# A new written order for the opening and the first 60 half blocks of an attention kernel with two expert layers

## The chip, the cores and the metric

The kernel runs as one program on one core of a Trainium2 chip. The metric is the device time of one execution in microseconds. Before the change it was 1586.91 us, the median of three runs that lay between 1586.84 and 1587.07 us.

The core has a matrix engine (PE in the profile), a vector engine (DVE), an activation engine (ACT), a general engine (POOL) and a queue that issues all transfers here (SP). Each engine works through its own instructions strictly in order, so the order in which the program lists them decides what waits behind what.

## The reference

The input is q, k, v of 8 batches, 8 heads, 576 tokens and 64 channels, and phi with 32 memory slots. The reference, cut to what is computed:

```
a    = softmax over the tokens of phi                # 8 x 8 x 576 x 32
k_m  = a^T k ;  v_m = a^T v                          # 32 rows for each head
attn = softmax over the slots of (q k_m^T / 8)
x    = attn v_m          -> 4608 tokens x 512
h    = x w_in  (512 -> 2048);  x = (h - tanh h) w_out      # layer 1
h    = x w_in2 (512 -> 2048);  x = elu(h) w_out2           # layer 2
```

The four weight matrices arrive as 64-bit floats.

## The kernel before

**Attention.** The work of 4 heads of one batch is a *unit*; there are 16 (u0 to u15), written as a generator `unit` (L251 to L370) that is advanced one step at a time. Its steps are in turn: the negated maximum of phi (DVE, L270); the exponential (ACT, L272); transposes aT and tail on PE (L278, L280) and their copies into tile `a` (L282 on DVE or L284 on ACT, L285 on ACT); the products km on PE (L294, L298); their scaling into kvs (L308 on ACT or L310 on DVE); the transposes kT (PE L317) and two copies (ACT L318, L320); the scores sc (PE L334) and their transposes (DVE L337); the maximum over the slots (DVE L341) and its subtraction (L342, POOL or DVE); the exponential (ACT L344); the sum, its reciprocal and the product (L346, L347 on DVE, L348 on POOL or DVE); a transpose (DVE L353); the split of the result into a high and a low part (L359 on POOL or L361 on ACT, then L362 on POOL or DVE); and the store of both (SP, L366 or L368). The result is the tile p, which layer 1 reads.

**Conversions.** Each weight matrix is brought from 64 to 32 bits in 16 pieces, 64 pieces in all (c0 to c63), each by a generator `conv` (L690) around `convert` (L176): a load of 512 KB (L693); a magnitude on ACT (L187); a clip (L189) on DVE or POOL; three steps of bit work on DVE (L192, L195, L198); and, save for the first matrix, a split into high (L204 on POOL or L206 on ACT) and low (L208 on POOL). The first matrix's pieces go into tiles named w1 in the lists below: c0 to c3 into the two that the first two half blocks need, c8 to c11 into the two that the next two need.

**Layer 1.** Tokens are cut into 16 blocks of 288 and the hidden width into groups of 256. Attention's last product and the first matrix are multiplied together first (`vw_unit`, L430: PE L440, then a copy on ACT L444 and a rest on DVE L445), so a hidden tile is p times vw (PE L458, H below). A *half block* is one block with one group; there are 128. One half block's chain: H, tanh and square (ACT L469, L473), a product (POOL L482), a polynomial (ACT L477, DVE L498), the difference h - tanh h (DVE L494), a mask (ACT L489) and a masked copy that chooses between the two (DVE L502), then the split (ACT L511, POOL L516). The second matrix follows some half blocks later: 12 matmuls for each x tile (PE L531) and a copy out of PSUM, on ACT (step X, L537) or on DVE (step Y, L539). Half blocks 0 and 1 use one vw, 2 and 3 the next, and so on.

**What sets the order.** Nothing is scheduled by a program here. A written list sets the order in which instructions are emitted: `BEGIN` lists steps up to the first half block (cN and uN advance a conversion or a unit; pN, qN and kN load phi, q, or k with v of unit N; v makes the first vw), and `SCRIPT` has one string for each of the 128 half blocks. Its letters are H (matmuls of the hidden tile), A, a, s, B, R, d, e, p (the chain: L469, L473, L477, L482, L489, L494, L498, L502), G and g (the split), X and Y (one x tile with its copy on ACT or DVE), V (a new vw), L and l (loads and stores), W (no work in most places). `POOLS` has a string for each unit that moves single steps to another engine, and `WHERE` a character for each conversion:

```python
on = lambda step: nc.gpsimd if step in where else nc.vector      # L254: letters s, m, l -> L342, L348, L362
if "e" in where: nc.vector.tensor_copy(a[:, :16]..., aT)          # L281, otherwise ACT
if "k" in where: nc.scalar.activation(kvs, twice, ...)            # L307, otherwise DVE
if "h" in where: nc.gpsimd.tensor_copy(t[:, 0], src)              # L358, otherwise ACT
hi_pool, where = where in ":GSB", {":": "."}.get(where, where.lower())   # L182: high part on POOL
m = a if where in "sb" else psum.tile(...)                        # L184: bit work in SBUF or in PSUM
(nc.gpsimd if where in "gb" else nc.vector).tensor_scalar(...)    # L189: the clip
```

The hidden tiles have two PSUM buffers, so H of a half block waits until the masked copy (L502) of the half block two before has read its tile; x tiles, vw and the attention units share three other PSUM buffers. Weight pieces have five load buffers. Layer 2 (L549 to L653) follows after about 780 us and is not touched by the change.

## Time and profile before

| | us |
|---|---|
| median of three runs | 1586.91 |
| the profiled execution | 1586.47 |
| its span, first to last instruction | 1584.5 |
| PE busy | 1532.8 (97% of the span) |
| DVE busy | 1103.8 (70%) |
| ACT busy | 892.0 (56%) |
| POOL busy | 720.4 (45%) |

The span is 1.97 us shorter than the profiled execution's time, and that execution is 0.44 us under the median. PE is busy nearly throughout, and of the 51.7 us in which it is not, most lie ahead of the layer 1 stream and in its first quarter. DVE's share of 70% is a mean: in the first slices of the page it is busy seven to nine tenths, in layer 2 five to six. A matmul row's end is modelled, and rows of one engine can overlap by some hundredths of a microsecond.

### The profile page before, as it was taken

The numbers are of one execution on the slowest core, as the hardware profiler recorded it, in microseconds if no ns is written. First come the engines' busy times: TensorE is split into PE (matmuls) and PEld (weight loads), VectorE is DVE, ScalarE is ACT, GpSimd is POOL, SyncE is SP. The second block draws the span as 40 slices with busy tenths as digits, with TensorE's granted clock in tenths as the row PEclk, the third lists the DMA queues.
The fourth block names the chain that finished last, engine by engine and source line by source line (L and its number), as shares of the span: only waits on it lengthen the run. The fifth ranks groups of instructions, "written<-read, shape, count | busy, mean of one in ns | idle before, by whom it ended". The sixth has DMA issues, their size and how long they took to land.

```text
span 1584.5 us, 27123 instructions
## 1 busy us (share of the span) xinstructions
PE 1532.8 (97%) x10406; PEld 1335.4 (84%) x10406; DVE 1103.8 (70%) x1615; ACT 892.0 (56%) x1603; POOL 720.4 (45%) x516
## 2 busy tenths in 40 slices
...
GB/s 324 290 145 247 250 227 212 291 240 220 179 169 169 222 227 226 219 190 179 320 269 107 69 51 67 41 67 54 69 65 40 93 41 71 49 67 40 40 1 27
DMA packets 118593, 232.84 MB, mean 147 GB/s; under 512 B 7616, under 2 KB 77248, under 8 KB 114368
## 3 DMA queue, kind: packets, MB, share of 16 engines
...
q10 hardware_dynamic: 288, 0.52, 0.1%
...
## 4 chain that ended last, share of the span: by engine, by line
PE 85%; DVE 7%; ACT 4%; issue 1%; POOL 1%; DMA 1%; SPq 0%; ACTq 0%; DVEq 0%; POOLq 0%
PE h_ps L591 25%; PE o_ps L638 25%; PE x_ps L531 21%; PE h_ps L458 11%; PE vw_ps L440 2%; DVE s L498 1%; PE km L294 1%; DVE s L502 1%; POOL v L482 1%; ACT t L469 1%; DVE cv_m L195 0%; DVE h_ps L494 0%; ACT u L473 0%; DVE w L198 0%; DVE cv_m L192 0%
## 5 line engine op out<-in xcount | busy, mean ns | idle before, releaser
L617 POOL TENSOR_TENSOR e<-hm,e 128x512 fp32r<-128x512 f32 x144 | 186.9, 1298 | 574.9 <-ACT e L616 531.8
L531 PE MATMUL x_ps<-g,w 128*128 128x288 f32 x3072 | 433.4, 296 | 6.5 <-ACT x L537 2.7
L531 PEld LDWEIGHTS x_ps<-g,w 128*128 128x128 f32 x3072 | 414.4, 188 | 14.2 <-ACT x L537 4.6
L591 PE MATMUL h_ps<-x,wi 128*128 128x512 f32 (+1 forms) x1920 | 422.2, 370 | 0.0
L638 PE MATMUL o_ps<-wo,e 128*128 128x512 f32 x1728 | 421.7, 393 | 0.0
L591 PEld LDWEIGHTS h_ps<-x,wi 128*128 128x128 f32 x1920 | 336.1, 188 | 66.2
L638 PEld LDWEIGHTS o_ps<-wo,e 128*128 128x128 f32 x1728 | 323.3, 188 | 73.1 <-POOL e L617 0.4
L602 ACT ACTIVATE t_ps<-hm 128x512 f32<-128x512 f32 x144 | 86.7, 602 | 500.6 <-DVE hm L601 500.6
L516 POOL TENSOR_TENSOR g<-s,g 128x576 fp32r<-128x576 f32 x128 | 199.3, 1557 | 106.3 <-ACT g L511 87.1
L482 POOL TENSOR_TENSOR v<-t,u 128x576 f32<-128x576 f32 x128 | 186.3, 1455 | 118.7 <-ACT u L473 109.7
L608 DVE SCALAR_TENSOR_TENSOR hm<-hm,t_ps 128x512 f32<-128x512 f32 x144 | 98.9, 687 | 200.6 <-ACT hm L603 200.6
L458 PE MATMUL h_ps<-p,vw 128*128 128x288 f32 x1536 | 233.3, 301 | 2.5 <-DMA p<-p_dram 0.8
L458 PEld LDWEIGHTS h_ps<-p,vw 128*128 128x128 f32 x1536 | 212.4, 190 | 17.6 <-issue 10.5
L601 DVE TENSOR_SCALAR hm<-h_ps 128x512 f32<-128x512 f32 x144 | 99.5, 691 | 128.2 <-PE h_ps L591 126.9
L498 DVE SCALAR_TENSOR_TENSOR s<-s,v 128x576 f32<-128x576 f32 x128 | 128.9, 1007 | 51.5 <-ACT big L489 30.5
L469 ACT ACTIVATE t<-h_ps 128x576 f32<-128x576 f32 x128 | 83.4, 652 | 67.8 <-issue 27.6
L502 DVE COPY_PREDICATED s<-big,h_ps 128x576 f32<-128x576 uint32 x128 | 106.3, 830 | 10.0 <-ACT big L489 1.3
L477 ACT ACTIVATE s<-u,bias 128x576 f32<-128x576 f32 x128 | 99.6, 778 | 13.2 <-POOL g L516 5.0
L494 DVE TENSOR_TENSOR h_ps<-h_ps,t 128x576 f32<-128x576 f32 x128 | 97.0, 758 | 13.7 <-ACT u L473 13.6
L609 DVE SCALAR_TENSOR_TENSOR hm<-hm,t_ps 128x512 f32<-128x512 f32 x144 | 98.9, 687 | 5.0
L610 DVE TENSOR_TENSOR hm<-hm,h_ps 128x512 f32<-128x512 f32 x144 | 98.9, 687 | 5.0
L489 ACT ACTIVATE big<-u,bias 128x576 f32<-128x576 f32 x128 | 98.2, 767 | 3.2 <-DVE s L502 3.0
...
## 6 DMA issues: line engine op xcount, KB each, us to landing
x_dram<-x SPq DMA_DIRECT2D x128, 288.0 KB, 2.7
xr<-x_dram SPq DMA_DIRECT2D x72, 512.0 KB, 3.7
p<-p_dram SPq DMA_DIRECT2D x62, 576.0 KB, 5.3
kv<-in_kv_dram SPq DMA_DIRECT2D x16, 1152.0 KB, 7.3
raw<-in_moe_w_in_dram SPq DMA_DIRECT2D x32, 512.0 KB, 4.6
raw<-in_moe_w_out_dram SPq DMA_DIRECT2D x32, 512.0 KB, 4.7
w_dram<-wst SPq DMA_DIRECT2D x32, 512.0 KB, 3.8
q<-in_q_dram SPq DMA_DIRECT2D x16, 576.0 KB, 5.6
```

What stands on the lines that cost most here:

```text
L458: nc.tensor.matmul(ps[:, j, :NB], lhsT=vw[a][:, kc, c0 + 128 * j:c0 + 128 * j + 128], rhs=p[:, kc, b, :], start=(k == 0), stop=(k == 5))
L469: nc.scalar.activation(t, w[0], ACTF.Tanh)
L477: self.nc.scalar.activation(s, u, ACTF.Square, bias=self.const["bias"][:, 0:1], scale=G_S)
L482: nc.gpsimd.tensor_tensor(v, t, u, op=ALU.mult)
L498: eng.scalar_tensor_tensor(s, s, G_B, v, op0=ALU.add, op1=ALU.mult)
L502: self.nc.vector.copy_predicated(s, big.bitcast(U32), d)
L516: self.nc.gpsimd.tensor_tensor(g[:, 1], s, r32(g[:, 0]), op=ALU.subtract)
L531: nc.tensor.matmul(ps, lhsT=wo[pg][a][:, j, 128 * dm:128 * dm + 128], rhs=self.g[n, pg][:, b, j, :], start=(k == 0), stop=(k == 11))
L591: nc.tensor.matmul(out, lhsT=w3[:, a, kc, 128 * j:128 * j + 128], rhs=x[:, b, kc, :], start=(i == 0), stop=(i == 11))
L601: nc.vector.tensor_scalar(hm, w[0], 0.0, None, op0=ALU.min)
L617: nc.gpsimd.tensor_tensor(e[:, 1], hm, r32(e[:, 0]), op=ALU.subtract)
L638: nc.tensor.matmul(acc, lhsT=e[:, a, jj, 128 * tg:128 * tg + 128], rhs=w4[:, b, j, :], start=(k == 0 and jj == 0 and (a, b) == (0, 0)), st ...
```

## The change

The list is written anew from `BEGIN` to the string of half block 59; half blocks 60 to 127 keep their strings. `POOLS` and `WHERE` are new too. No function changes. Every half block keeps its letters of the chain; steps of units and conversions stand in other places, some x copies change between X and Y, and some steps change engine. Cut to the two tables and the first lines of the lists:

```diff
-BEGIN = ("c0 p1 c0 q1 p0 u1 u0 u0 c1 u0 k1 u1 p2 c0 k0 c1 c2 u1 c0 c2 u2 c1 q0 c2 u1 u0 u1 c3 c4 c6 c2 u2 u0 "
+BEGIN = ("c2 p1 p0 c2 u1 u1 u0 k1 c0 u0 c2 u1 c0 c0 c2 c0 c1 u0 k0 p2 c1 q0 q1 c1 c1 u2 u1 u1 u0 c3 u2 c4 u3 "
...
-SCRIPT = ("c6 W u2 c4 H A a d s V u0 R G Y v X L c5 B u3 l e p g c6 c7",
+SCRIPT = ("W c6 c4 Y H A a Y v L R G c5 s V u3 B d e p c5 g l",
...
-POOLS = ("sl", "mks", "lmsk", "msl", "sl", "sk", "", "e", "lk", "ls", "msk", "mlk", "m", "mlsek", "lk", "lk")
-WHERE = "..s.gb.g:ggb.g:.g.s..g:.g:g...............................gss..."
+POOLS = ("slhm", "mks", "lmske", "msl", "slkh", "sk", "h", "kmh", "", "shk", "msk", "lkh", "mkeh", "msekh", "lkme", "lk")
+WHERE = "b...gb:g.GgB.g:sg.:..gG.g:g..G............................gss.g."
```

What this does to the instructions shows in their order on single engines. In the names below a number tells one tile from another, and the same tile has another number in the two kernels.

SP, the first eleven transfers of the program, before (raw is a conversion's piece, kv_139 unit 1's and kv_157 unit 0's k and v; phi_164, phi_171 and phi_196 belong to units 1, 0 and 2):

```order
L693 DMA raw_162<-in_moe_w_in_dram 128x512
L248 DMA phi_164<-in_phi_dram 128x576
L248 DMA q_169<-in_q_dram 128x1152
L248 DMA phi_171<-in_phi_dram 128x576
L693 DMA raw_180<-in_moe_w_in_dram 128x512
L248 DMA kv_139<-in_kv_dram 128x2304
L248 DMA phi_196<-in_phi_dram 128x576
L248 DMA kv_157<-in_kv_dram 128x2304
L693 DMA raw_204<-in_moe_w_in_dram 128x512
L248 DMA phi_223<-in_phi_dram 128x576
L248 DMA q_230<-in_q_dram 128x1152
```

The same place in the changed kernel (phi_166 is unit 0's phi, phi_221 and phi_234 those of units 2 and 3):

```order
L693 DMA raw_162<-in_moe_w_in_dram 128x512
L248 DMA phi_164<-in_phi_dram 128x576
L248 DMA phi_166<-in_phi_dram 128x576
L248 DMA kv_139<-in_kv_dram 128x2304
L693 DMA raw_179<-in_moe_w_in_dram 128x512
L693 DMA raw_206<-in_moe_w_in_dram 128x512
L248 DMA kv_157<-in_kv_dram 128x2304
L248 DMA phi_221<-in_phi_dram 128x576
L248 DMA q_226<-in_q_dram 128x1152
L248 DMA q_228<-in_q_dram 128x1152
L248 DMA phi_234<-in_phi_dram 128x576
```

Unit 0's phi and unit 1's k and v now stand ahead of both q and of the second piece of weights, and two pieces of weights stand ahead of unit 0's k and v. The next two transfers are unit 2's k and v and a fourth piece of weights (raw_286 before, raw_291 now).

DVE, right behind the second L341 (the slot maximum of unit 1), before (s0 and s1 are the scores of units 0 and 1; cv_m_379 is a conversion):

```order
L286 TENSOR_SCALAR rs_226<-rs_226 128x1
L287 RECIPROCAL rs_226<-rs_226 128x1
L270 TENSOR_REDUCE nmax_352<-phi_223 128x1
L346 TENSOR_REDUCE smax_315<-s0_120 128x18
L347 RECIPROCAL smax_315<-smax_315 128x18
L348 TENSOR_TENSOR s0_120<-s0_120,smax_315 128x18x32
L445 TENSOR_TENSOR vw_363<-vw_ps_364,vw_362 128x256
L445 TENSOR_TENSOR vw_363<-vw_ps_365,vw_362 128x256
L189 TENSOR_SCALAR cv_m_379<-cv_m_379 128x512
L192 TENSOR_SCALAR cv_m_379<-cv_m_379 128x512
L346 TENSOR_REDUCE smax_332<-s1_121 128x18
L347 RECIPROCAL smax_332<-smax_332 128x18
```

The same place in the changed kernel (cv_m_312 is the conversion of raw_291):

```order
L189 TENSOR_SCALAR cv_m_312<-cv_m_312 128x512
L192 TENSOR_SCALAR cv_m_312<-cv_m_312 128x512
L346 TENSOR_REDUCE smax_338<-s0_120 128x18
L347 RECIPROCAL smax_338<-smax_338 128x18
L195 SCALAR_TENSOR_TENSOR cv_m_312<-raw_291,cv_m_312 128x512
L198 SCALAR_TENSOR_TENSOR w1_200<-raw_291,cv_m_312 128x512
L346 TENSOR_REDUCE smax_359<-s1_121 128x18
L347 RECIPROCAL smax_359<-smax_359 128x18
L445 TENSOR_TENSOR vw_377<-vw_ps_378,vw_376 128x256
L445 TENSOR_TENSOR vw_377<-vw_ps_379,vw_376 128x256
```

Unit 0's product L348 has left DVE (it is on POOL now), unit 2's L286 and L287 and unit 3's L270 have moved ahead of the piece shown, and a whole conversion stands ahead of the first two L445.

DVE, behind the transposes L353 in half block 2, up to the last bit step of the fourth w1 tile, before (s_656 is half block 2's chain, w1_759 the fourth w1 tile):

```order
L310 TENSOR_SCALAR kvs_742<-km_672,rs_439 128x256
L502 COPY_PREDICATED s_656<-big_660,h_ps_642 128x576
L270 TENSOR_REDUCE nmax_754<-phi_436 128x1
L192 TENSOR_SCALAR cv_m_745<-cv_a_744 128x512
L195 SCALAR_TENSOR_TENSOR cv_m_745<-raw_638,cv_m_745 128x512
L198 SCALAR_TENSOR_TENSOR w1_759<-raw_638,cv_m_745 128x512
L539 COPY x_787<-x_ps_774 128x288
L337 STREAM_TRANSPOSE s1_121<-sc_789 128x9x32
L337 STREAM_TRANSPOSE s1_121<-sc_790 128x9x32
L192 TENSOR_SCALAR cv_a_728<-cv_a_728 128x512
L195 SCALAR_TENSOR_TENSOR cv_a_728<-raw_665,cv_a_728 128x512
L198 SCALAR_TENSOR_TENSOR w1_759<-raw_665,cv_a_728 128x512
```

The same place in the changed kernel:

```order
L502 COPY_PREDICATED s_670<-big_674,h_ps_657 128x576
L192 TENSOR_SCALAR cv_m_681<-cv_a_680 128x512
L195 SCALAR_TENSOR_TENSOR cv_m_681<-raw_624,cv_m_681 128x512
L198 SCALAR_TENSOR_TENSOR w1_759<-raw_624,cv_m_681 128x512
L337 STREAM_TRANSPOSE s1_121<-sc_778 128x9x32
L337 STREAM_TRANSPOSE s1_121<-sc_779 128x9x32
L192 TENSOR_SCALAR cv_a_695<-cv_a_695 128x512
L195 SCALAR_TENSOR_TENSOR cv_a_695<-raw_676,cv_a_695 128x512
L198 SCALAR_TENSOR_TENSOR w1_759<-raw_676,cv_a_695 128x512
```

L310 (now on ACT), L270 (moved up) and L539 (moved down) are gone from between; half block 2's L494, which stood a little ahead of the piece, has moved further up.

## Rows read from the trace of the kernel before

**Rows 1.** Windows: busy us of each engine, PE's granted clock, DMA share, GB/s

```profile
0.00:20.00 20.00, 8.09 (x100) 5.46 (x100) 8.49 (x19) 7.05 (x15) 0.82 (x8) 1.00 0.89 342
20.00:100.00 80.00, 59.10 (x629) 46.12 (x628) 74.20 (x136) 55.54 (x115) 48.63 (x41) 0.87 0.71 266
100.00:440.00 340.00, 326.01 (x3118) 295.50 (x3120) 283.33 (x432) 268.38 (x510) 213.12 (x150) 1.00 0.66 225
440.00:1585.00 1145.00, 1139.60 (x6575) 988.34 (x6563) 737.81 (x1031) 561.00 (x965) 457.86 (x318) 1.00 0.34 112
```

**Rows 2.** Timeline of PE: start, us, instruction, idle before it and its releaser

```profile
41.34 1.08 PE L294 MATMUL km<-kv,a 128*32 128x128 f32 x32 [2.13 <-DVE vw L445]
...
57.64 1.08 PE L440 MATMUL vw_ps<-w,vm 64*32 64x256 f32 x8 [5.25 <-DVE w L198]
...
62.60 0.69 PE L317 MATMUL kT_ps<-ident,kvs 128*128 128x128 f32 x2 [0.95 <-DVE vw L445]
...
69.26 0.63 PE L278 MATMUL aT<-ident,phi 128*128 128x128 f32 x4 [0.79 <-DVE x L539]
...
71.83 0.64 PE L440 MATMUL vw_ps<-w,vm 64*32 64x256 f32 x8 [0.62 <-DVE w L198]
```

**Rows 3.** Timeline of DVE, opening (columns as above)

```profile
5.05 0.75 DVE L270 TENSOR_REDUCE nmax<-phi 128x1 f32<-128x576 f32 x1 [4.16 <-DMA phi<-in_phi_dram]
...
22.29 0.84 DVE L337 STREAM_TRANSPOSE s<-sc 128x288 f32<-128x288 f32 x2
...
24.70 0.75 DVE L341 TENSOR_REDUCE smax<-s 128x18 f32<-128x576 f32 x1
...
40.87 0.75 DVE L445 TENSOR_TENSOR vw<-vw_ps,vw 128x256 fp32r<-128x256 f32 x2
...
59.84 0.69 DVE L198 SCALAR_TENSOR_TENSOR w<-raw,cv_m 128x512 uint32<-128x512 uint32 x1
...
71.08 0.69 DVE L198 SCALAR_TENSOR_TENSOR w<-raw,cv_a 128x512 uint32<-128x512 uint32 x1
```

**Rows 4.** Timeline of ACT, opening: magnitudes of the first and third piece loaded

```profile
4.31 0.62 ACT L187 ACTIVATE cv_m<-raw 128x512 f32<-128x512 f32 x1 [2.29 <-DMA raw<-in_moe_w_in_dram]
...
16.36 0.67 ACT L187 ACTIVATE cv_a<-raw 128x512 f32<-128x512 f32 x1 [1.61 <-DMA raw<-in_moe_w_in_dram]
```

**Rows 5.** DMA issues, 0 to 60 us: count, KB each, median us to landing

```profile
kv<-in_kv_dram SPq DMA_DIRECT2D x6, 1152.0 KB, 7.5
raw<-in_moe_w_in_dram SPq DMA_DIRECT2D x8, 512.0 KB, 6.6
...
q<-in_q_dram SPq DMA_DIRECT2D x5, 576.0 KB, 7.1
phi<-in_phi_dram SPq DMA_DIRECT2D x7, 288.0 KB, 5.2
```

**Rows 6.** Groups of DVE by line and form, 0 to 800 us: busy, mean ns, idle before

```profile
L494 DVE TENSOR_TENSOR h_ps<-h_ps,t 128x576 f32<-128x576 f32 x128 | 97.0, 758 | 13.7 <-ACT u L473 13.6
...
L539 DVE COPY x<-x_ps 128x288 f32<-128x288 f32 x77 | 34.5, 449 | 20.4 <-PE x_ps L531 20.2
...
L348 DVE TENSOR_TENSOR s<-s,smax 128x576 f32<-128x576 f32 x9 | 7.1, 792 | 0.3
...
L362 DVE TENSOR_TENSOR phl<-phl 128x576 fp32r<-128x576 f32 x5 | 5.9, 1180 | 3.3 <-ACT phl L361 3.3
...
L310 DVE TENSOR_SCALAR kvs<-km,rs 128x256 f32<-128x256 f32 x7 | 3.3, 469 | 1.3 <-PE km L298 1.3
...
L282 DVE COPY a<-aT 128x512 f32<-128x512 f32 x2 | 1.4, 684 | 0.2 <-PE aT L278 0.2
```

**Rows 7.** Groups of POOL by line and form, 0 to 800 us

```profile
L204 POOL CAST wst<-cv_a 128x512 fp32r<-128x512 f32 x2 | 1.2, 623 | 0.0
```

**Rows 8.** Timeline of PE: a half block that waits for L502

```profile
249.51 1.85 PE L458 MATMUL h_ps<-p,vw 128*128 128x288 f32 x12 [0.63 <-DVE s L502]
```

**Rows 9.** Instructions of L498, 0 to 440 us: ns min, median, max

```profile
L498 DVE SCALAR_TENSOR_TENSOR s<-s,v x62: 737/758/2024, 43.5 to 437.0; 128x576 f32<-128x576 f32 x62
```

4 lines of the change are left out of this document (2 added, 2 removed), and 120 rows, old and new, of the table SCRIPT.

## The prediction

> **What bounds the kernel now.** I read the windows first. From 440 us on PE is busy 1139.6 of 1145 us, so whatever happens earlier is carried unchanged to the end; the time is decided by how much PE stands idle before. That is 11.9 us in the first 20 us, 20.9 us from 20 to 100 us and 14.0 us from 100 to 440 us [rows 1]: 46.8 us, of which the change can take or add a part. Between 20 and 100 us DVE is busy 74.2 of 80 us, and PE's granted clock is 0.87, a mean of its two levels, 2.4 and 1.2 GHz. PE's timeline then says what it waits for there: 2.13 us for a vw rest (L445), 5.25 us for the last bit step of the third w1 tile (L198), 0.95 us for the next L445, then 0.79 us and 0.62 us [rows 2]. All are late DVE instructions. So the opening is a queue of DVE work: its length up to a gate and the moment at which it starts without gaps give the time. Behind 72 us PE is nearly full, and the last look is at the middle, where no single wait is large.
>
> **The start.** DVE's first work waits 4.16 us for phi [rows 3], so the landing of transfers counts. The first piece of weights is read on ACT at 4.31 us, the third at 16.36 us [rows 4]; by the order on SP, 288, 576, 288, 512, 1152, 288, 1152 and 512 KB lie between [rows 5], 4768 KB in 12.05 us, so 396 KB/us. With that rate the new order lands, after the first piece: unit 1's phi at 5.0, unit 0's phi at 5.8 (7.3 before), unit 1's k and v at 8.7 (11.3 before), two pieces of weights at 10.0 and 11.3, unit 0's k and v at 14.2, unit 2's phi at 14.9, both q at 16.3 and 17.8, unit 3's phi at 18.5, unit 2's k and v at 21.4, the fourth piece at 22.7. DVE works in order, and the last thing it has to wait for before the scores is unit 3's phi at 18.5. Behind it stand L270 (0.75 [rows 3]), L282 (0.68 [rows 6]), the pair L286, L287, and the four transposes L337 with two L341. Those six took from 22.29 to 24.70 + 0.75 = 25.45 us before, 3.16 us [rows 3]. So the second L341 ends at 18.5 + 0.75 + 0.68 + 3.16 = 23.1 us; the pair, some tenths, stood behind it before and now stands ahead, and I leave it out on both sides. Gain 2.35 us. Bounds: 0, if unit 3's phi, now behind both q, lands 2.4 us later; 3.8, if unit 3's phi is no wait and 1.45 us (one q of 576 KB at that rate) of it fall away.
>
> **First gate, the second vw.** Before, DVE needs from 25.45 to 40.87 + 0.75 = 41.62 us [rows 3] for the fourth L445. The two orders differ in that stretch by an L270 (0.75) and an L348 (0.79 [rows 6]) that are gone, and by an L189 and an L192 that are there early (0.69 each, as L198 of the same 512 columns [rows 3]): -0.16 us. Gate at 23.1 + 16.17 - 0.16 = 39.1 us, 2.5 us earlier.
>
> **Second gate, the third w1 tile**, on which PE waits 5.25 us. Before it is reached at 59.84 + 0.69 = 60.53 us, 18.91 us later. Now the L189 and L192 are already done (-1.38), and an L270 (+0.75) and half block 2's L494 (+0.76 [rows 6]) stand ahead of it instead: +0.13 us, so 58.15 us, 2.4 us earlier. Here PE has waited, so its stream gains 2.4 us in full.
>
> **Third gate, the fourth w1 tile**, before at 71.08 + 0.69 = 71.77 us [rows 3]. In this stretch an L494 (0.76), an L310 (0.47), an L270 (0.75) and an L539 (0.45) are gone [rows 3, 6], 2.4 us, so DVE would come 4.8 us earlier. But PE idles only 0.79 + 0.62 = 1.41 us between the gates [rows 2]; more it cannot gain. I take 1.0 of it, between 0 and 1.4. What is late then is PE's own stream.
>
> **From 72 to 440 us.** The order on PE hardly changes there, only units' products and x tiles swap places. The edits of engine net, by half block 43, DVE: +2 L282, +3 L362, +4 L539, -3 L310, -2 L348, -2 L189 (0.69 as above), that is 1.4 + 3.5 + 1.8 - 1.4 - 1.6 - 1.4 = +1.3 us by the rows' means [rows 6]; the rest of the list's places makes it some 2 to 3 us that DVE does earlier than before. Its cover is DVE's 56.7 us of idle time between 100 and 440 us [rows 1]. ACT loses nine copies L361 and POOL takes nine L359, which the trace before doesn't show. Its nearest row is POOL's L204, 0.62 us for 512 columns [rows 7], so 0.70 for 576 and 6 us in all, the upper end of what it can cost as a wait; the lower is -6 us, if ACT was what these waited for. Neither engine is full: POOL idles 127 us and ACT 72 us in that stretch [rows 1], so I take 0. For the 14.0 us of PE idle, made of many waits of about 1 us, I take -0.2 us, with bounds of -3 and +4: one wait more or less in each block of four half blocks is about that.
>
> **Sum.** 2.4 + 1.0 + 0.2 = 3.6 us less. The profiled execution took 1586.47 us (span 1584.5), so it would take 1582.9; its median stands 0.44 us higher, so 1583.3 us.
>
> **A rule that speaks against it.** L498 reads two tiles in SBUF; its median is 758 ns and its longest 2024 ns [rows 9], so something holds up a few. The Trainium skill, "SBUF — State Buffer", section "Who interferes with whom", states that VectorE instructions with two SBUF inputs contend with GpSimd instructions that read SBUF, and that the one that comes later is blocked for the other's whole length. By that rule every instruction moved to POOL can stop DVE; the trace agrees so far as the spread goes, but a median 21 ns above the minimum of 737 says that most are not touched.
>
> **The rivals.** *A, the gain is given back before 440 us.* When PE comes 3 us earlier, H of a half block meets L502 of the one two before, which DVE does not do earlier, since it has 2 to 3 us more to do. One such wait, 0.63 us, is there already [rows 8]. Five more of that size take 3.2 us: 1586.5 us. For it: DVE is 83% busy in that stretch. Against: 17% idle is 56.7 us, most of it waiting for H itself.
>
> *B, the fourth piece of weights comes late (slower).* Its magnitude L187 now stands on ACT ahead of both softmax exponentials L344, and its clip on DVE right behind the second L341; in before these exponentials stood ahead of it. So a late transfer now holds up attention itself. It must land by 25.45 + 0.16 - 0.62 = 25.0 us for no loss; I have 22.7. Each microsecond later costs one in the gates. It is the last of 7296 KB behind the first piece; at 290 KB/us it lands at 4.31 + 7296/290 = 29.5 us, 4.5 us too late, and PE is not made up for it later: 1591.4 us. It decides (over 0.2%) from 28.2 us on. Against: even the 342 GB/s of the first 20 us, the start in it [rows 1], 334 KB/us, land it at 26.2 us, 1.2 us too late.
>
> *C, POOL blocks DVE (slower).* POOL has 12 instructions more by half block 43: two L189, two L204, one L208, one L348, nine L359, less three L362. If each holds up one of DVE's two-input instructions for 0.62 us [rows 7], 7.4 us go and 3.6 come: 1590.7 us. It decides from 0.57 us each. Against it stands the median in rows 9; for it the longest, 1.27 us over the median.
>
> *D, the change does nothing*, since the waits of the opening move to another releaser at the same time: 1586.9 us.
>
> **How the numbers follow.** What a measurement of this kernel can tell from no change is about 0.2%, 3.2 us. The forecast has 0.46: three of its terms are lengths of a queue that I can count. With the half of its cases that reach over it, it goes from 1579 to 1583.7, and all of it counts as faster. A has 0.26 and D 0.08, together the 0.34 for no change. B has 0.11 and C 0.09, 0.20 for slower. The range, 1578.5 to 1589, takes the forecast with its bounds (-8.1 at the far end of the opening and the middle together), A, D and the nearer half of B and C.
>
> **What would show it.** In the profile after: the second L341 ends near 23.1 us; the fourth L445 near 39; L198 of the third w1 tile near 58 and PE's wait of about 5 us ahead of its vw still there; the vw of the fourth w1 tile without a wait; PE's idle time up to 100 us down from 32.8 to about 29.4 us, and from 100 to 440 us still about 14. ACT's L187 of the fourth piece without an idle time past 25 us. It is wrong if the idle time between 100 and 440 us moves by more than 3 us, if ACT waits for the fourth piece past 25 us, or if L498's median rises.

## The result and the profile after

The changed kernel takes 1559.4 us (median of four runs, 1559.13 to 1560.03) against 1586.88 us for the kernel before beside it: 27.5 us less, ratio 0.9827 with a 95% interval of 0.981 to 0.9844. The forecast was 1583.3 us, 3.6 us less. The direction was right, the size was not.

The windows after, over the stretches of [rows 1]:

```profile
0.00:20.00 20.00, 10.43 (x108) 6.75 (x108) 11.02 (x23) 8.50 (x20) 1.43 (x9) 1.00 0.91 356
20.00:100.00 80.00, 66.72 (x707) 53.18 (x706) 73.96 (x137) 55.05 (x112) 52.84 (x48) 0.91 0.76 287
100.00:440.00 340.00, 338.01 (x3257) 312.17 (x3256) 296.74 (x458) 280.78 (x531) 230.39 (x169) 1.00 0.69 232
440.00:1557.00 1117.00, 1113.07 (x6342) 963.56 (x6341) 715.58 (x1000) 539.25 (x928) 441.19 (x306) 1.00 0.34 111
```

PE's idle time is the stretch less its busy time. It falls from 11.9 to 9.6 us, from 20.9 to 13.3 us and, between 100 and 440 us, from 14.0 to 2.0 us: 22.0 us in all. The span fell by 26.8 us (1584.5 to 1557.7). Most of the rest, 4.6 us, is in PE's busy time, 1532.8 before and 1528.2 us after, with the same matmuls. A busy PE row can hide a stall: over half blocks 9 to 63, what each matmul's start-to-start time has above the median of its tile, the visible gaps taken off, sums to about 45 us before and 39 us after, some 5.8 us less.

Where the time goes is seen best from the moment at which a half block's first matmul of H (L458) starts on PE. Half block 0 starts 2.5 us earlier than before, half block 3 5.8, half block 9 9.6, half block 18 14.6, half block 33 21.5, half block 63 26.7 us; from there on the lead is constant to half block 126 (26.8). So 9.6 us come ahead of half block 9 (103.9 us after) and 17.1 us between half blocks 9 and 63, 11.9 of them up to half block 33. Up to half block 9 PE's idle time falls by 10.9 us (33.7 to 22.9) and its busy time rises by 1.3 us, so the opening is not won by the higher granted clock of its windows (0.91 against 0.87 between 20 and 100 us).

PE's timeline after: the gates of the opening, and then the only three gaps of 0.3 us or more between 100 and 440 us.

```profile
39.02 1.59 PE L458 MATMUL h_ps<-p,vw 128*128 128x288 f32 x10 [0.68 <-DVE vw L445]
...
54.08 0.91 PE L440 MATMUL vw_ps<-w,vm 64*32 64x256 f32 x8 [4.18 <-DVE w L198]
56.17 1.08 PE L440 MATMUL vw_ps<-w,vm 64*32 64x256 f32 x8 [1.18 <-DVE w L198]
...
64.48 1.44 PE L440 MATMUL vw_ps<-w,vm 64*32 64x256 f32 x16 [0.42 <-ACT a L284]
...
223.34 1.85 PE L531 MATMUL x_ps<-g,w 128*128 128x288 f32 x12 [0.77 <-DVE rs L286]
...
265.87 1.86 PE L531 MATMUL x_ps<-g,w 128*128 128x288 f32 x12 [0.52 <-DVE rs L286]
...
269.12 1.08 PE L294 MATMUL km<-kv,a 128*32 128x128 f32 x32 [0.37 <-DVE s L337]
```

Before, 17 gaps of that size stood between 100 and 440 us, among them the one at 249.51 [rows 8], which is gone. The gates of [rows 2] are still waits for L198 where 5.25 us stood, and short ones elsewhere. Two rows of PE before, which the prediction did not use, belong beside them:

```profile
60.58 1.08 PE L440 MATMUL vw_ps<-w,vm 64*32 64x256 f32 x8 [1.85 <-DVE w L198]
...
82.51 3.62 PE L531 MATMUL x_ps<-g,w 128*128 128x288 f32 x24 [0.86 <-DVE x L539]
```

DVE's timeline after answers to [rows 3]: unit 3's phi, the scores, the second L341, the fourth L445, half block 1's L498, and L198 of the third and fourth w1 tile.

```profile
19.16 0.75 DVE L270 TENSOR_REDUCE nmax<-phi 128x1 f32<-128x576 f32 x1 [1.03 <-DMA phi<-in_phi_dram]
...
21.45 0.85 DVE L337 STREAM_TRANSPOSE s<-sc 128x288 f32<-128x288 f32 x2 [0.65 <-PE sc L334]
...
23.88 0.75 DVE L341 TENSOR_REDUCE smax<-s 128x18 f32<-128x576 f32 x1
...
38.55 0.75 DVE L445 TENSOR_TENSOR vw<-vw_ps,vw 128x256 fp32r<-128x256 f32 x2
...
47.93 0.75 DVE L498 SCALAR_TENSOR_TENSOR s<-s,v 128x576 f32<-128x576 f32 x1
...
55.43 0.69 DVE L198 SCALAR_TENSOR_TENSOR w<-raw,cv_m 128x512 uint32<-128x512 uint32 x1
...
64.54 0.69 DVE L198 SCALAR_TENSOR_TENSOR w<-raw,cv_a 128x512 uint32<-128x512 uint32 x1
```

ACT after, the magnitude of the fourth piece of weights ([rows 4] had the first and third), and DVE's clip behind it:

```profile
24.37 0.62 ACT L187 ACTIVATE cv_m<-raw 128x512 f32<-128x512 f32 x1 [3.51 <-DMA raw<-in_moe_w_in_dram]
...
25.02 0.70 DVE L189 TENSOR_SCALAR cv_m<-cv_m 128x512 f32<-128x512 f32 x1 [0.40 <-ACT cv_m L187]
```

L498 after, 0 to 440 us ([rows 9]: 737/758/2024):

```profile
L498 DVE SCALAR_TENSOR_TENSOR s<-s,v x67: 736/759/2020, 41.3 to 434.7; 128x576 f32<-128x576 f32 x67
```

### The profile page after: what moved, and what is told of

It reads as the page before. It is cut to its first block, busy times and chain, and to the rows that moved or that the text cites. A ratio compares the mean times of both kernels' runs of the same rounds, so it can differ in the third digit from the quotient of the medians.

```text
span 1557.7 us, 27109 instructions
## 1 busy us (share of the span) xinstructions
PE 1528.2 (98%) x10406; PEld 1335.7 (86%) x10406; DVE 1097.3 (70%) x1615; ACT 883.6 (57%) x1588; POOL 725.8 (47%) x531
## 4 chain that ended last, share of the span: by engine, by line
PE 94%; DVE 3%; DMA 1%; ACT 1%; issue 1%; ACTq 0%; SPq 0%; DVEq 0%
PE x_ps L531 26%; PE h_ps L591 26%; PE o_ps L638 25%; PE h_ps L458 13%; PE vw_ps L440 2%; PE km L294 1%; DMA raw<-in_moe_w_in_dram 1%; PE sc L334 0%; PE x_ps L214 0%; DVE s L498 0%; PE aT L278 0%; PE km L298 0%; DVE cv_m L195 0%; DVE cv_m L192 0%; DMA phi<-in_phi_dram 0%
## 5 line engine op out<-in xcount | busy, mean ns | idle before, releaser
L516 POOL TENSOR_TENSOR g<-s,g 128x576 fp32r<-128x576 f32 x128 | 198.0, 1548 | 106.0 <-ACT g L511 85.2
L458 PE MATMUL h_ps<-p,vw 128*128 128x288 f32 x1536 | 233.2, 301 | 0.8 <-DVE vw L445 0.7
L482 POOL TENSOR_TENSOR v<-t,u 128x576 f32<-128x576 f32 x128 | 185.7, 1451 | 95.8 <-ACT u L473 70.7
L458 PEld LDWEIGHTS h_ps<-p,vw 128*128 128x128 f32 x1536 | 212.3, 190 | 16.2 <-issue 12.9
L498 DVE SCALAR_TENSOR_TENSOR s<-s,v 128x576 f32<-128x576 f32 x128 | 125.2, 978 | 44.6 <-ACT big L489 27.9
L469 ACT ACTIVATE t<-h_ps 128x576 f32<-128x576 f32 x128 | 83.4, 652 | 65.0 <-issue 19.8
L502 DVE COPY_PREDICATED s<-big,h_ps 128x576 f32<-128x576 uint32 x128 | 106.4, 831 | 9.0 <-ACT big L489 1.2
L477 ACT ACTIVATE s<-u,bias 128x576 f32<-128x576 f32 x128 | 99.5, 777 | 10.5 <-POOL g L516 3.7
L494 DVE TENSOR_TENSOR h_ps<-h_ps,t 128x576 f32<-128x576 f32 x128 | 97.0, 758 | 10.9 <-ACT u L473 10.9
```

The costliest lines, as they stand in the source:

```text
L458: nc.tensor.matmul(ps[:, j, :NB], lhsT=vw[a][:, kc, c0 + 128 * j:c0 + 128 * j + 128], rhs=p[:, kc, b, :], start=(k == 0), stop=(k == 5))
L477: self.nc.scalar.activation(s, u, ACTF.Square, bias=self.const["bias"][:, 0:1], scale=G_S)
L482: nc.gpsimd.tensor_tensor(v, t, u, op=ALU.mult)
L498: eng.scalar_tensor_tensor(s, s, G_B, v, op0=ALU.add, op1=ALU.mult)
L502: self.nc.vector.copy_predicated(s, big.bitcast(U32), d)
L516: self.nc.gpsimd.tensor_tensor(g[:, 1], s, r32(g[:, 0]), op=ALU.subtract)
```

## The experiments

Seventeen kernels ran; nothing of the computation is left out in any of them. The expectations name theories. L: it is the opening's lead that moves the middle. M: the engines of the steps and their places in the list are matched, and neither does it alone. B: the middle's waits are for the three PSUM buffers that x tiles, vw and units share. Later names are told in the expectations themselves. "Opening" is `BEGIN` and the strings of half blocks 0 to 9, "rest" the strings from half block 10 on; the new list reaches one string further than "The change" says, since that of half block 60 differs too. Each kernel has its time, its ratio to the kernel before in the same series with the 95% interval (that kernel took 1586.41 to 1586.89 us in the five series), PE's idle time between 100 and 440 us, and how much later (+) or earlier (-) half blocks 9 and 63 start than before. The last three columns are read from one execution of each kernel, which lay within 2.0 us of the median, save h1's, 4.0 us above it.

| kernel | us | ratio [95%] | idle 100 to 440 | half block 9 | half block 63 |
|---|---|---|---|---|---|
| before | 1586.88 | 1 | 14.0 | 0 | 0 |
| changed | 1559.4 | 0.9827 [0.981, 0.9844] | 2.0 | -9.6 | -26.7 |
| e1 | 1577.22 | 0.9938 [0.9923, 0.9953] | 9.9 | -6.0 | -9.1 |
| e2 | 1599.34 | 1.0081 [1.0066, 1.0096] | 22.1 | +1.7 | +11.8 |
| e3 | 1588.60 | 1.0011 [1.0001, 1.0021] | 21.1 | -9.7 | +0.4 |
| e4 | 1573.68 | 0.9916 [0.9901, 0.9931] | 5.1 | +1.6 | -12.8 |
| f1 | 1578.29 | 0.9948 [0.9933, 0.9963] | 13.0 | -8.9 | -8.0 |
| f3 | 1574.25 | 0.9921 [0.9904, 0.9937] | 5.7 | +1.4 | -10.8 |
| f2 | 1573.55 | 0.9917 [0.9897, 0.9937] | 9.1 | -9.3 | -13.3 |
| g1 | 1567.14 | 0.9876 [0.9862, 0.9891] | 6.1 | -7.0 | -19.5 |
| g2 | 1562.59 | 0.985 [0.9835, 0.9864] | 3.5 | -9.5 | -23.4 |
| h1 | 1630.45 | 1.0279 [1.0262, 1.0296] | 33.5 | +5.5 | +39.3 |
| h2 | 1624.97 | 1.0241 [1.0226, 1.0256] | 30.3 | +5.0 | +32.1 |
| h3 | 1603.90 | 1.0107 [1.0092, 1.0122] | 26.0 | -8.1 | +10.4 |
| i1 | 1587.42 | 1.0003 [0.9994, 1.0012] | 13.9 | +0.3 | +0.7 |
| i3 | 1586.86 | 0.9999 [0.999, 1.0008] | 13.5 | +0.3 | +0.9 |
| i2 | 1588.18 | 1.0008 [0.9999, 1.0017] | 15.1 | -0.8 | +0.9 |
| i4 | 1585.62 | 0.9993 [0.9985, 1.0002] | 12.9 | +0.6 | -0.8 |
| i5 | 1586.40 | 0.9996 [0.9987, 1.0005] | 12.6 | +0.3 | -0.1 |

**e1, the new lists with the old engines of the units.** The edit, against the changed kernel:

```diff
-POOLS = ("slhm", "mks", "lmske", "msl", "slkh", "sk", "h", "kmh", "", "shk", "msk", "lkh", "mkeh", "msekh", "lkme", "lk")
+POOLS = ("sl", "mks", "lmsk", "msl", "sl", "sk", "", "e", "lk", "ls", "msk", "mlk", "m", "mlsek", "lk", "lk")
```

> The new list and the new places of conversions' steps, but the table of the units' engines (POOLS) of the kernel before. Theory P, places: the 12 us of PE idle that vanished between 100 and 440 us went because steps stand in other places, so that the three shared PSUM buffers and the hidden tile are free in time; then this keeps most of the gain, 1559 to 1565 us, with PE idle of 2 to 6 us from 100 to 440 us. Theory E, engines: they went because ACT lost 9 us of work; then most of the middle's gain is gone, 1572 to 1580 us, PE idle of 8 to 14 us there. Theory L, the lead of the opening: nothing changes here beyond the opening, 1559 to 1562 us.

Of 27.5 us, 9.7 are left, in the range of theory E. The engines of the units' steps are worth 17.8 us in the new places: 3.6 ahead of half block 9 and 14.0 between half blocks 9 and 63, where the prediction had priced them at zero.

**e2, the old lists with the new engines.** The reverse, against the kernel before (the `WHERE` characters of the opening's conversions stay old):

```diff
-POOLS = ("sl", "mks", "lmsk", "msl", "sl", "sk", "", "e", "lk", "ls", "msk", "mlk", "m", "mlsek", "lk", "lk")
-WHERE = "..s.gb.g:ggb.g:.g.s..g:.g:g...............................gss..."
+POOLS = ("slhm", "mks", "lmske", "msl", "slkh", "sk", "h", "kmh", "", "shk", "msk", "lkh", "mkeh", "msekh", "lkme", "lk")
+WHERE = "..s.gb.g:ggb.g:sg.:..gG.g:g..G............................gss.g."
```

> The list of the kernel before in full, with the new table of the units' engines and the new engines of the conversions from c14 on. Theory P: no gain or a loss, 1583 to 1592 us. Theory E: 1565 to 1575 us, PE idle of 2 to 6 us from 100 to 440 us. Theory L: as before within 3 us, 1584 to 1590 us.

The same engines make the old lists 12.5 us slower (1599.34 against 1586.88). None of the theories' ranges has this time. The engines are good or bad only with the places.

**e3 and e4, the opening alone and the rest alone, both with the new engines** (in e4 the `WHERE` characters of the opening's conversions are old). In e3 `BEGIN` and the strings 0 to 9 are new and the strings from 10 on old; e4 is the mirror image:

```diff
-SCRIPT = ("c6 W u2 c4 H A a d s V u0 R G Y v X L c5 B u3 l e p g c6 c7",
+SCRIPT = ("W c6 c4 Y H A a Y v L R G c5 s V u3 B d e p c5 g l",
...
```

```diff
-          "W l H A a d u7 L B R s X u5 X V G e g p",
+          "W l H V A a B X u5 R d G u7 X s L e g p",
...
```

(String 0, the first of e3's new ones, and string 10, the first of e4's.)

> The new list up to half block 9, from half block 10 on the old one (all units and conversions stand at the same step there in both), new engines. Theories P and E of the middle: the opening brings what the trace shows at half block 9, 9.6 us, and the middle is the old one: P 1575 to 1579 us with 12 to 15 us of PE idle from 100 to 440 us; E 1560 to 1565 us, since the engines are the new ones. Theory L: the lead of the opening makes the middle's waits vanish, 1559 to 1565 us.

> The old list up to half block 9, the new one for half blocks 10 to 59, new units' engines, and the new conversions' engines from c14 on. Theories P and E: the opening is the old one, the middle's gain of 17 us comes in full, 1567 to 1573 us, PE idle of 2 to 5 us from 120 to 440 us. Theory L: the middle's waits are back, 1580 to 1587 us.

e3 has the whole opening gain, -9.7 us at half block 9, and loses all of it by half block 63: with the new engines in old places PE idles 21.1 us in the middle. Yet e4 has the middle's gain without that lead: it is 4.5 us late at half block 12, where old opening and new rest meet, and gains 17.3 us from there to half block 63. So L is wrong. No theory's range had e3's time, which speaks for M.

**f1 and f3, the halves with the engines that belong to them.** f1 is e3 with the old engines from unit 6 and conversion 14 on; f3 has the old opening with its engines and the new rest with its own:

```diff
-POOLS = ("slhm", "mks", "lmske", "msl", "slkh", "sk", "h", "kmh", "", "shk", "msk", "lkh", "mkeh", "msekh", "lkme", "lk")
-WHERE = "b...gb:g.GgB.g:sg.:..gG.g:g..G............................gss.g."
+POOLS = ("slhm", "mks", "lmske", "msl", "slkh", "sk", "", "e", "lk", "ls", "msk", "mlk", "m", "mlsek", "lk", "lk")
+WHERE = "b...gb:g.GgB.g:.g.s..g:.g:g...............................gss..."
```

> The new list up to half block 9 with the new engines of the units 0 to 5 and of the conversions up to c13; everything behind it as in the kernel before. Theory P (places and engines of the middle remove its waits by themselves): the opening's 9.6 us of lead arrive at half block 10 and the old middle neither gives nor takes, 1575 to 1579 us, 13 to 15 us of PE idle from 100 to 440 us. Theory L (the lead of the opening removes the middle's waits): 1559 to 1566 us. Theory R (the lead is given back: the old places were fitted to the old opening, and PE that comes earlier meets the same readers later): 1582 to 1588 us, over 18 us of idle there.

> The old list up to half block 9 with the old engines of the units 0 to 5 and of the conversions up to c13; behind it the new list and the new engines. Theory P: the middle's 17 us come in full, 1568 to 1572 us, 1 to 4 us of PE idle from 120 to 440 us. Theory L: 1583 to 1588 us. If places and engines only pay with the new opening's progress of the units, something between, 1573 to 1580 us.

The windows of e3 and f1, 100 to 440 us, one row each:

```profile
100.00:440.00 340.00, 318.86 (x3022) 289.38 (x3028) 281.06 (x424) 261.08 (x495) 213.64 (x158) 0.99 0.65 220
```

```profile
100.00:440.00 340.00, 327.00 (x3100) 297.44 (x3100) 286.57 (x438) 271.76 (x515) 215.45 (x154) 0.99 0.66 222
```

f1's PE works 8.1 us more than e3's in the stretch, from engine letters alone, and its lead is 8.9 us at half block 9 and still 8.0 at half block 63. So a lead is kept where the middle is left alone, and it does not shorten the middle either. f3 is 6.2 us late at half block 12, where old opening and new rest meet, and from there to half block 63 it gains 17.0 us, the changed kernel's middle. The two parts nearly add up: 8.0 and 17.0 us against 26.7.

**f2, the changed kernel with the old engines from unit 6 on.**

```diff
-POOLS = ("slhm", "mks", "lmske", "msl", "slkh", "sk", "h", "kmh", "", "shk", "msk", "lkh", "mkeh", "msekh", "lkme", "lk")
+POOLS = ("slhm", "mks", "lmske", "msl", "slkh", "sk", "", "e", "lk", "ls", "msk", "mlk", "m", "mlsek", "lk", "lk")
```

> The changed kernel, but the units 6 to 15 have their old engines; the opening is the new one in full. Theory M, matched: a place in the list and the engine of the step there only pay together; the old engines in the old middle cost 17 us over the changed kernel, and in the new places they cost nearly as much, 1568 to 1578 us, 8 us or more of PE idle from 100 to 440 us. Theory P, places alone: 1559 to 1563 us.

From half block 9 to 63 it gains 4.0 us. So the middle moves by +0.9 us with neither (f1), -4.0 with new places and old engines of the units (f2), +10.1 with new engines alone (e3, and e2 as well), -17.1 with both. That is M, with one blur: in f2 the conversions from c14 on keep their new engines, so what these add by themselves is not told apart.

**g1 and g2, one kind of edit taken back.** g1 strikes the letter h from `POOLS` (the high part goes back from POOL L359 to ACT L361); g2 gives the x copies of the changed kernel the old sequence of X and Y (15 letters):

```diff
-POOLS = ("slhm", "mks", "lmske", "msl", "slkh", "sk", "h", "kmh", "", "shk", "msk", "lkh", "mkeh", "msekh", "lkme", "lk")
+POOLS = ("slm", "mks", "lmske", "msl", "slk", "sk", "", "km", "", "sk", "msk", "lk", "mke", "msek", "lkme", "lk")
```

```diff
-SCRIPT = ("W c6 c4 Y H A a Y v L R G c5 s V u3 B d e p c5 g l",
+SCRIPT = ("W c6 c4 Y H A a X v L R G c5 s V u3 B d e p c5 g l",
...
```

> The changed kernel, but the first copy of a unit's split stays on ACT (L361) in all units, as it was; so the nine L359 on POOL are gone and 5.7 us of ACT work are back. Theory E (engines): the units' copies on POOL are what ACT was relieved of, so a good part of the loss of the run with all old units' engines (17.8 us over the changed kernel) shows here, 1565 to 1575 us. Theory P: 1558 to 1562 us.

> The changed kernel, but each x tile is copied out by the engine that did it before (X or Y as in the old list, 13 or so swapped, at the new places). If the engines of x copies hold the middle's gain, since x tiles and the units share three PSUM buffers: 1566 to 1575 us with 6 us or more of PE idle from 100 to 440 us. If places of the units' and conversions' steps hold it: 1558 to 1563 us.

The letter h, which eight units have (nine instructions L359, as unit 0's copy is made in two parts), is worth 7.7 us in the changed kernel (1567.14 less 1559.4), 2.6 of them ahead of half block 9; the x copies 3.2 us. Neither is the cause by itself.

**h1 to h3, a try at B: one PSUM buffer more.** A conversion's bit work in SBUF (`WHERE` s, S or b) leaves the conversions' PSUM bank free from conversion 14 on. h1 does only that, on the kernel before, as the control; h2 gives the free bank to the second vw tile besides; h3 is the changed kernel with both.

```diff
-WHERE = "..s.gb.g:ggb.g:.g.s..g:.g:g...............................gss..."
+WHERE = "..s.gb.g:ggb.gSsbssssbSsbSbsssssssssssssssssssssssssssssssbsssss"
...
-        ps = [self.misc.tile([128, 512], F32, tag="m", name="vw_ps") for _ in range(2)]
+        ps = [self.misc.tile([128, 512], F32, tag="m", name="vw_ps"), (self.own or self.misc).tile([128, 512], F32, tag="c" if self.own else "m", name="vw_ps")]
```

> Control for the next run: the kernel before, with the bit steps of all conversions from c14 on in SBUF instead of PSUM, so that the conversions' PSUM bank stands empty from half block 10 on. The places in the list are the old ones. DVE's bit steps get a little shorter or meet POOL; 1583 to 1592 us, 12 to 18 us of PE idle from 100 to 440 us.

> The same, and the second of the two vw tiles goes into the empty bank from half block 10 on, so x tiles, units and vw press less on the three shared PSUM buffers. Theory B, shared buffers: most waits of PE between 100 and 440 us are for a reader that has not freed one of these three buffers; then at least a third of them goes, 4 to 9 us less than the control. Theory N, readers' data (inputs, not buffers): within 2 us of the control.

> The changed kernel with both of these edits. Its PE idles only 2 us between 100 and 440 us, so theory B leaves little to gain: 1556 to 1561 us. If bit steps in SBUF disturb the new places: 1562 to 1568 us.

The control ruined the test: h1, expected at 1583 to 1592 us, is 44.0 us slower than the kernel before in its series (1586.41). DVE's last bit step, groups by line and form, before (one operand, cv_m, in PSUM) and in h1 (both in SBUF):

```profile
L198 DVE SCALAR_TENSOR_TENSOR cv_a<-raw,cv_m 128x512 uint32<-128x512 uint32 x46 | 31.6, 687 | 1.6
```

```profile
L198 DVE SCALAR_TENSOR_TENSOR cv_a<-raw,cv_a 128x512 uint32<-128x512 uint32 x43 | 66.1, 1538 | 1.5
```

One of them in h1, with the POOL instruction that was running:

```profile
195.34 1.44 POOL L482 TENSOR_TENSOR v<-t,u 128x576 f32<-128x576 f32 x1 [0.92 <-ACT u L473]
...
195.46 1.87 DVE L198 SCALAR_TENSOR_TENSOR cv_a<-raw,cv_a 128x512 uint32<-128x512 uint32 x1
```

POOL's product ends at 196.78 us and the bit step at 197.33: it took 0.69 us at least in this kernel, and here it finishes 0.55 us after POOL does. h3, with the same bit work, is 44.5 us slower than the changed kernel, where 1556 to 1568 us had been expected. The extra bank gave 5.5 us (h1 to h2), so shared buffers do cost time there, but on a kernel that was slowed otherwise, and PE's idle time in the middle fell by a tenth and not by the third that theory B had named; B is neither shown nor refuted by this.

**i1 and i3, one unit step, one engine.** The largest gap of the middle before, 1.61 us at 165.02, was then followed on every engine. The timelines of the kernel before, in order of time:

```profile
157.71 1.44 POOL L516 TENSOR_TENSOR g<-s,g 128x576 fp32r<-128x576 f32 x1
157.73 2.02 DVE L498 SCALAR_TENSOR_TENSOR s<-s,v 128x576 f32<-128x576 f32 x1 [0.75 <-POOL v L482]
...
162.44 0.69 ACT L361 ACTIVATE phl<-phl 128x576 fp32r<-128x576 f32 x1 [3.55 <-DVE phl L353]
...
163.16 0.76 DVE L362 TENSOR_TENSOR phl<-phl 128x576 fp32r<-128x576 f32 x1 [0.75 <-ACT phl L361]
163.84 0.79 DVE L502 COPY_PREDICATED s<-big,h_ps 128x576 f32<-128x576 uint32 x1
164.52 0.45 DVE L539 COPY x<-x_ps 128x288 f32<-128x288 f32 x1
...
165.02 0.33 PE L280 MATMUL tail<-ident,phi 64*64 64x64 f32 x4 [1.61 <-DVE x L539]
```

One unit's steps hold up two rows: ACT stands 3.55 us ahead of unit 6's L361, with L469 of the next half block behind it, and DVE stands 0.75 us ahead of L362, with L502 and the x copy behind it. A third delay stands ahead of both: L498 takes 2.02 us, where those of i1 and i3 take 0.76, and ends 0.60 us behind the end of POOL's L516. i1 moves L362 to POOL (letter l for unit 6), i3 moves L361 to POOL (letter h):

```diff
-POOLS = ("sl", "mks", "lmsk", "msl", "sl", "sk", "", "e", "lk", "ls", "msk", "mlk", "m", "mlsek", "lk", "lk")
+POOLS = ("sl", "mks", "lmsk", "msl", "sl", "sk", "l", "e", "lk", "ls", "msk", "mlk", "m", "mlsek", "lk", "lk")
```

> The kernel before with one letter more: unit 6's product L362 goes from DVE to POOL. In the trace before, DVE stands 0.75 us for unit 6's high part (ACT L361 at 162.44) with that L362, then 0.76 us in it, and behind it stand L502 of half block 15 and the x copy L539 at 164.52, on which PE waits 1.61 us at 165.02. Theory R (the middle's idle time is single late readers of the three shared PSUM buffers, held up by what stands ahead of them in their engine's row): L539 ends some 1.4 us earlier, PE's gap at 165.02 shrinks from 1.61 to about 0.2 us, half blocks 16 and later start 1.0 to 1.5 us earlier, and the lead is kept: 1585.4 to 1585.9 us. Rival L (a lead in the middle is swallowed by the next waits): half block 18 is earlier and half block 63 is not, 1586.9 us. Rival C (a product on POOL holds up DVE's instructions with two inputs in SBUF): 1587 to 1588 us.

> The kernel before with one letter more: unit 6's high part goes from ACT (L361) to POOL (L359). In the trace before ACT stands idle 3.55 us ahead of that L361 (waiting for DVE's L353), and L469 of the next half block stands behind it. POOL is idle at that moment and needs 0.67 us by the trace after, so L362 on DVE starts at the same time. Theory R: L502 and L539, which stand behind that L362, come no earlier, so PE's 1.61 us at 165.02 stay: 1586.5 to 1587.0 us, though ACT's row is freed by 3 us. Rival Q (what counts is that ACT's row is freed): half block 18 starts 1 us or more earlier, 1585 to 1586 us.

i1's timelines:

```profile
162.12 0.44 DVE L539 COPY x<-x_ps 128x288 f32<-128x288 f32 x1
162.31 1.42 POOL L362 TENSOR_TENSOR phl<-phl 128x576 fp32r<-128x576 f32 x1 [4.24 <-ACT phl L361]
163.69 1.41 POOL L516 TENSOR_TENSOR g<-s,g 128x576 fp32r<-128x576 f32 x1
...
165.14 0.78 ACT L477 ACTIVATE s<-u,bias 128x576 f32<-128x576 f32 x1 [1.83 <-POOL g L516]
...
166.51 0.76 DVE L498 SCALAR_TENSOR_TENSOR s<-s,v 128x576 f32<-128x576 f32 x1 [3.95 <-POOL v L482]
...
167.50 1.20 PE L334 MATMUL sc<-q,kT 64*32 64x288 f32 x16 [1.66 <-ACT x L537]
```

The x copy comes 2.4 us earlier and the gap at the tail is gone, as theory R had it. But POOL's L516 now stands behind L362, ACT's L477 waits 1.83 us for it, and the next x copy, on ACT behind L477, makes PE wait 1.66 us: the same gap under another name. Nothing is gained: half block 15 starts 0.4 us later than before, 17 1.3 us earlier and 18 0.8 us later. That is a lead swallowed by the next wait, as rival L has it, only sooner than L named. The time lies in C's range, but C's reason is not there: DVE has nothing but the x copy to do while POOL works on L362, and its next product, L498, waits for POOL's L482 and takes its usual 0.76 us. i3's timelines:

```profile
158.01 0.76 DVE L498 SCALAR_TENSOR_TENSOR s<-s,v 128x576 f32<-128x576 f32 x1 [0.74 <-POOL v L482]
...
162.11 1.43 POOL L516 TENSOR_TENSOR g<-s,g 128x576 fp32r<-128x576 f32 x1
162.18 1.97 DVE L362 TENSOR_TENSOR phl<-phl 128x576 fp32r<-128x576 f32 x1 [0.76 <-POOL phl L359]
...
165.26 0.33 PE L280 MATMUL tail<-ident,phi 64*64 64x64 f32 x4 [1.57 <-DVE x L539]
```

Here L469 starts 2.9 us earlier (160.17 against 163.03), and the gap stays. R has the time right, but not for its reason. L362 does not start when it did but 1.0 us earlier, since L516, now behind L359 on POOL, no longer holds up L498 (0.76 us instead of 2.02). It holds up L362 instead, which takes 1.97 us instead of 0.76 and ends 0.61 us behind L516. So DVE's row is late again, and what the freed row of ACT is worth without this collision i3 does not show.

**i2, the letter h of the eight units in the old places.** The edit, against the kernel before:

```diff
-POOLS = ("sl", "mks", "lmsk", "msl", "sl", "sk", "", "e", "lk", "ls", "msk", "mlk", "m", "mlsek", "lk", "lk")
+POOLS = ("slh", "mks", "lmsk", "msl", "slh", "sk", "h", "eh", "lk", "lsh", "msk", "mlkh", "mh", "mlsekh", "lk", "lk")
```

> The kernel before with the letter h for the nine units that have it in the changed kernel, all else as before. In the changed kernel taking the h away costs 7.8 us. Theory M (engines and places are matched): in the old places the nine letters give little, between 2 us less and 3 us more, 1585 to 1590 us, and half block 63 starts between 2 us earlier and 3 us later. Rival Q (freeing ACT's row is worth the same wherever the steps stand): 1579 us, and half block 63 starts about 7 us earlier.

1.0008, its interval just reaching 1: no gain, where the same eight letters are worth 7.7 us in the new places. M, again.

**i4 and i5, the same unit's place.** Only the string of half block 15 changes; i5 has unit 6's h besides.

```diff
-          "W V H u7 A a s G X d B R L e c16 u6 u6 X u6 p l g",
+          "W V H u7 A a s G X u6 d u6 B R L e c16 X p u6 l g",
```

> The kernel before with one string of the list changed, that of half block 15: unit 6's three steps (product L346 to L348, transposes L353, split L361 and L362) stand some instructions further up, the product ahead of L494, the transposes ahead of L498, and the masked copy L502 ahead of L362. All engines as before. The runs on unit 6 showed that one engine relieved leaves PE's gap of 1.6 us where it is or hands it to the next x copy, since DVE's, ACT's and POOL's rows are late by the same unit step. Theory R2 (the step's place holds up all three rows, so a place 2 us earlier takes the gap away): the gap of 1.61 us at 165 us falls under 0.5 us and no other appears before half block 18, which starts 1.2 to 2.0 us earlier; the lead is kept to half block 63: 1584.8 to 1585.7 us. Rival E (place and engine are both needed): half block 18 at most 0.5 us earlier, 1586.3 to 1587 us. Rival L (kept for some half blocks only): half block 18 earlier, half block 63 not, 1586.8 us.

> The same string for half block 15, and unit 6's high part on POOL (L359) besides. Theory R2: as the run with the places alone, 1584.8 to 1585.7 us, since the places do it. Rival E (place and engine are both needed, as the whole tables had it): half block 18 starts 1.2 to 2.0 us earlier here and not with the places alone. Rival L as there: half block 18 earlier, half block 63 not, 1586.8 us.

DVE in i4, the unit's product and the end of that piece:

```profile
156.95 2.01 DVE L348 TENSOR_TENSOR s<-s,smax 128x576 f32<-128x576 f32 x1
...
161.83 0.75 DVE L362 TENSOR_TENSOR phl<-phl 128x576 fp32r<-128x576 f32 x1
162.49 0.46 DVE L539 COPY x<-x_ps 128x288 f32<-128x288 f32 x1
```

L362 no longer waits and the x copy is 2.0 us earlier than before, with the opening 0.6 us late in this execution. The collision is not gone: it hits L348 (2.01 us) and not L498 (0.71). What is gone is DVE's idle time, 0.75 us ahead of L498 and 0.75 ahead of L362 before; from the product to the x copy DVE now works without a gap. PE has no gap of 0.3 us or more between 156 and 170 us, in i5 neither. From half block 15 to 18, i4 goes from +0.6 to -1.1 us and i5 from +0.3 to -1.2: 1.7 and 1.5 us, the whole gap. At half block 63 i4 still has 1.4 of its 1.7 us, i5 has lost 1.1 of 1.5 between half blocks 24 and 33. In the total neither is told from the kernel before (i4 1.27 us less, its interval just reaching 1). So here the place alone does it (R2), E is refuted for this gap, and of what is won in one place some is kept (i4) and most lost behind it in the other run (i5, rival L's case).

## Why the prediction was wrong

**The start.** The second L341 was put at 23.1 us and ended at 23.88 + 0.75 = 24.63. Unit 3's phi came 0.7 us later than estimated (its L270 starts at 19.16), and the scores, which I had not counted as a wait, cost 0.65 us on DVE. The fourth piece landed at about 24.3 us, not 22.7, so the rate was some 365 KB/us (7296 KB in 20.0 us) instead of 396. That is still inside rival B's limit of 25.0 us: L344 follows at 25.03 us. DVE stood 0.40 us for it all the same, ahead of the clip at 25.02.

**First gate.** The fourth L445 was put at 39.1 and ended at 39.30 us, but by two errors that cancel. The start was 1.5 us late, and the stretch behind it 1.3 us shorter than my sum. The sum priced each step at its own length; before, one of them, L195, had been held up by POOL, and so had L498 at the second gate. The timelines of the kernel before:

```profile
38.31 1.37 POOL L208 TENSOR_TENSOR w<-cv_a,w 128x512 fp32r<-128x512 f32 x1 [2.44 <-ACT w L206]
38.57 1.66 DVE L195 SCALAR_TENSOR_TENSOR cv_a<-raw,cv_a 128x512 uint32<-128x512 uint32 x1
...
50.73 1.28 POOL L208 TENSOR_TENSOR w<-cv_a,w 128x512 fp32r<-128x512 f32 x1
50.81 1.82 DVE L498 SCALAR_TENSOR_TENSOR s<-s,v 128x576 f32<-128x576 f32 x1 [0.91 <-POOL v L482]
```

Both DVE instructions start within 0.3 us behind one of POOL's and end 0.55 and 0.62 us behind its end. The same two after take 0.69 and 0.75 us: POOL's L208 stands elsewhere. The Trainium skill, "SBUF — State Buffer", section "Who interferes with whom", says that of a VectorE instruction with two SBUF inputs and a GpSimd one that reads SBUF the later is blocked for the other's length; these rows agree. I had weighed it by L498's median, which tells nothing of the few that are hit, and two of these stood ahead of a gate.

**Second gate.** L198 of the third w1 tile was put at 58.15 and ended at 55.43 + 0.69 = 56.12 us, 4.4 us earlier than before instead of 2.4. Most of the difference is that L498: 1.07 us of its length and the 0.91 us that it had waited for POOL.

**Third gate.** The cap was wrong. I let PE gain no more than 0.79 + 0.62 us between the gates, took 1.0, and left out the 0.95 us that [rows 2] shows for the kT at 62.60; and I took PE as full behind 72 us, while it idled 0.86 us at 82.51 and 1.5 us more up to 112 us. These waits sum to 4.7 us, and after only 0.9 us of waits stand between the second gate and half block 9; PE's busy rows there, with two transposes fewer, are 1.4 us shorter. That is 5.2 us where I had 1.0, and with the 2.0 us of the second gate the 6.2 us that the opening gave beyond my 3.4.

**72 to 440 us: the step that failed.** "For the 14.0 us of PE idle, made of many waits of about 1 us, I take -0.2 us, with bounds of -3 and +4." From half block 9 to 63 it was -17.1 us, 11.3 in gaps and some 5.8 in stalls inside busy rows. Two sentences led there. "Neither engine is full: ... so I take 0" priced an engine move by the engines' idle time: e1 shows 14.0 us for the units' engine letters in this stretch, and e2, in the old places and with the conversions' letters from c14 on, 10.1 us the other way. And the bounds, one wait more or less in each block, took the waits for a floor: i4 removes one of them with one string and no engine. (The sum of DVE's edits has a slip too: by half block 43 DVE has one L348 less and not two, which makes +2.1 us of +1.3; no term hangs on it.)

What a wait is made of is shown for one: a unit's step stands where its operand is late, and everything behind it in that row, the chain of a half block and an x copy with its buffer, is late with it, on DVE, ACT and POOL alike; a collision with POOL adds 1.3 us on DVE. Relieving one engine hands the wait to the next (i1) or the collision to the next instruction (i3); the place earlier fills DVE's idle time and removes the wait (i4). In the changed kernel unit 6's steps also come earlier in the list, and its timelines show no wait at that point:

```profile
146.17 0.67 POOL L359 CAST phl<-phl 128x576 fp32r<-128x576 f32 x1
...
147.89 0.66 ACT L469 ACTIVATE t<-h_ps 128x576 f32<-128x576 f32 x1
148.59 0.78 DVE L362 TENSOR_TENSOR phl<-phl 128x576 fp32r<-128x576 f32 x1
149.44 0.46 DVE L539 COPY x<-x_ps 128x288 f32<-128x288 f32 x1
...
151.35 0.33 PE L280 MATMUL tail<-ident,phi 64*64 64x64 f32 x4
```

That the other gaps went the same way is argued from this one, not shown: only the sums of places and engines were tested on them. Collisions with POOL changed less in sum, and what they are worth to PE was not tested by itself: between 100 and 440 us, DVE instructions other than L445 that took over 0.25 us more than the shortest of their kind held 22.8 us too much in 30 cases before and 18.0 us in 24 after. How much of PE's 17.1 us is for shared PSUM buffers and how much for late operands stays open (h1 to h3).

**The rivals.** A did not happen: the lead of the opening is kept (f1), and in the changed kernel it grows. Its counter-argument read DVE's idle time wrongly: between 100 and 440 us no wait of DVE is for H itself, and the most, 19.4 us, stand ahead of L498 for the POOL and ACT steps of the chain. B did not, by 0.6 us. D, no change, did not. C did not: L498's median is 759 ns, and its 128 instructions take 978 ns in the mean against 1007. Of the signs named, the third gate without an L198 wait came, PE's wait ahead of the third tile's vw is still there with 4.18 us, and L445 near 39 came by the two errors. The second L341 (24.6 instead of 23.1), L198 of the third tile (56.1 instead of 58) and PE's idle time up to 100 us (22.9 instead of 29.4) did not come. The idle time of the middle, "still about 14", was 2.0, and it had been named as what would make the forecast wrong.
